# Linear attention into a gated feed-forward layer, one core: first batch's queries by chunk, tail numerators in column halves, PSUM banks from a table, a new order

## The chip, the cores and the metric

The kernel runs on one core of a Trainium2 chip. What counts is the device time of one execution in microseconds (us). Smaller is better.

## What is computed

The reference, cut to what matters:

```python
batch, n_heads, seq, head_dim = (8, 8, 576, 64); d_feat = 128
def phi(x):
    proj = np.einsum('bhsd,df->bhsf', x, w_phi)
    proj = proj - np.max(np.abs(proj), axis=-1, keepdims=True)
    return np.concatenate([np.exp(proj), np.exp(-proj)], axis=-1)
q_p, k_p = (phi(q), phi(k))
kv = np.einsum('bhsf,bhsd->bhfd', k_p, v)
z = np.sum(k_p, axis=2)
num = np.einsum('bhsf,bhfd->bhsd', q_p, kv)
den = np.einsum('bhsf,bhf->bhs', q_p, z)[..., None] + 1e-06
x = (num / den) as [4608 tokens, 512]
gate = np.maximum(x @ w_gate, 0.0); val = x @ w_val      # [512, 1536]
out = gate * val @ w_out                                   # [1536, 512]
```

## The kernel before

**The pieces.** A batch has 576 tokens and 8 heads. The first 512 tokens of a batch are its main part, four chunks of 128. The last 64 are its tail, and the tails of two batches that follow each other share one tile of 128 rows (a unit "u", four in all). The feed-forward layer then runs in nine groups of 512 tokens: one for each batch's main part (0 to 7) and one for the tails (8).

**Keys.** A key tile is turned (head_dim into the partitions), for batches 0 and 1 by TensorE with a copy (`kT`, `kTc`), later by a transposing DMA on SyncE's queue (`turn`). TensorE multiplies it with `w_phi` in two halves of 64 rows that sit in the two halves of the array (`rows_of`, L312). VectorE takes the largest magnitude (`km`, L319), ScalarE the two exponentials (`ke`, L368) and the factor of the row (`kk`, L379), and GpSimd or VectorE scales the values by it (`vs`, L328). TensorE then sums over tokens (`kv`, L486, and L509 for batches 0 and 1), and a copy brings the result to SBUF (`kvc`, L422).

**Queries.** The projection is made twice: with features in the partitions for the exponentials (`qc`, L549, then `qe`, L567), and with tokens in the partitions for the row maximum (`qr`, L312, then `qm`). From them come the numerators and denominators, three groups of heads for each chunk: `n` on TensorE (L597), `nt` (L616) and `nu` (L628) on VectorE, the reciprocal and the division (`xu`, L635 and L642, the latter on GpSimd unless the order says otherwise). The result is turned into `xT` by TensorE and a copy (`xT`, `xc`, L662) for batches 0 and 1, by a DMA after that (`xd`, L650).

For a tail unit, the numerators are made once with the first batch's `kv` and once with the second's, each time for all 128 rows and into a PSUM bank of its own. VectorE then reads 64 rows of each, so that `nt` and `nu` are two instructions of 64 rows each.

**Feed-forward.** One step makes 128 hidden columns for 512 tokens: four matmuls for the value (`fv`, L734) and a copy (L749), four for the gate (`fg`, L734), and VectorE's product of the two (L756). Twelve steps make `h`, then `fo` (L791) multiplies by `w_out`, a copy (L805) and a store follow. Group 0 starts before its batch is complete: its first four hidden blocks are made by halves of 256 tokens (`FIRST`), each with a bank, a copy and a product of its own.

**The order.** Every piece is an "atom" that registers itself with a number. `ORDER` lists all numbers, and `run` issues them in that order; an accent after a number takes the other engine (`alt`), and `zN` puts in N matmuls of zeros. Instructions of one engine run in the order in which they are issued, so the string sets each engine's own order and that of the queues on which GpSimd and SyncE issue DMAs. The eight PSUM banks come from one pool of eight buffers, taken in turn. `val_sb` has four buffers, `h2` one.

Of the kernel before, what the change touches and what calls it, by code (L numbers as in the profile page):

```python
# [11 lines left out]
ALU = mybir.AluOpType  # L12
# [4 lines left out]

K_CUTS = [[4, 8, 16, 24, 32], [8, 16, 24, 32]]
# [5 lines left out]


ORDER = """7 z3 82 92 93 83' 84 87 94 86 8 0 98 102 85 89 90 91 88 103 z1 104 96 97 108 105 95 107 106 z1 112
113 109 99 101 110' 111 122 114 115 123' 124 127 118 116 132 1 117 133 119 120 121 125 100' 128 z1
148 149 129 126 187 10 134 188 151 153 155 137 2 131 156 135 158 160 142 130 196 144 136 200 198
150 154 236 139 141 237 143 140 246 247 157 159 152 29 161 162 226 190 192 54 138 256 257 175 163
194 176 164 165 189 145 147' 191 266 177 146 3 267 193 4 169 170 166 167 171 168 195 199 181 178  # L30
182 321 214 5 172 179 183 180 184 201 197 217 215 11 220 221 218 222 219 208 9 322' 216 173 174'
282 283 223 209 185 186' 202 203 238 227' 210 205 206 204 207 240 211 1092 1093 1094 224 225' 239
1095 1096 324 328 228 229 242 212 213' 1097 326 232 1098 1099 1100 1101 1102' 231 6 1103 1104 1105
1106 1107 230 241 1108 243 268 269 270 271 273 258 274 272 261 248 251 260 249 253 255 254 1109 252
259 263 39 1110' 1111 1112' 264 1113 1114 275 250 233 1115 1116' 1117 290 361 262 363 265 292 365
279 280' 281' 323 327 291 295 293 1118 1119 294 1120' 1121 284 325 288 330 30 51 332 334 234 245
244 235 276 277 329 333 285 287 13 40 278' 289 1122 1123 351 296 1124 335 352 353 309 312 310 311
# [3 lines left out]
347' 32 55 61 371 372 307 308' 16 1134 63 388 398 402 399 391 400 383 385 1135' 1136 389 1137 401  # L41
42 403 1138' 405 393 367 368 369 395 392 394 390 1139 1140 1141 33 1142' 1143 1144' 17 43 424 426
428 384 418 454 458 420 1145 456 1146' 422 1147 1148 460 462 464 465 419 421 423 508 512 509 1149
# [4 lines left out]
502 1163 1164 1165' 534 536 538 564 529 531 523 1166 1167 568 503 570 476 574 566 533 569 571 1168  # L48
573 515 514 516 572 18 1169 1170 535 517 539 528 537 530 488 491 524 492 525 526 527 532 1171' 1172
1173 1174 1175 489 563 66 67 565 20 45 504 34 505 506 69 19 44 1176 1177 493 36 1178' 495 1179 567  # L50
507' 1180' 1181 494 490 590 555 496 497 1182' 593 575 591 68 587 588 589 540 1183 592 594 541 542
# [3 lines left out]
585 586 643 1199 1200 46 72 657 661 659 646 650 647 616 619 1201' 608 648 618 649 651 652 609 1202  # L55
# [3 lines left out]
675 676 716 717 741 1217 672 673 677 718 719 704 705 706 707 708 709 47 1218' 1219 1220 1221 1222  # L59
669 670 721 722 723 671 1223 1224 674 720 724 740 615 1225 1226 683 684 685 756 757 725 746 747 749  # L60
53 766 770 768 678 679 743 759 1227 1228 750 1229 1230' 710 711 712 760 713 758 761 763 714 680 681
# [58 lines left out]
def kernel(  # L120
# [594 lines left out]
    for b in range(B):  # L715
# [3 lines left out]
        if b % 2 == 1:  # L719
            q_tails(b // 2)  # L720


    t_count = [0]

    def ffn(g):
        st = {}
# [137 lines left out]
```

## Time and profile before

| | |
|---|---|
| three runs | 379.0, 384.38 and 378.77 us, median 379.0 |
| profiled execution, first to last instruction | 377.4 us |
| TensorE (PE) busy | 368.1 us, 98% |
| VectorE (DVE) busy | 290.7 us, 77% |
| ScalarE (ACT) busy | 213.1 us, 56% |
| GpSimd (POOL) busy | 151.3 us, 40% |
| granted TensorE clock, mean | 0.995 |

The profile tells of one execution. PE rows are matmuls, PEld rows weight loads. In a timeline row stand the start, the length from the first start to the last end, the engine, the line, what is written and read, and the count. One matmul's own length is its latency (about 0.38 us for 512 columns): the next one starts long before that has passed, so the rate is read from distances between starts. A line of the stretches (windows) has the bounds, the length, the busy time and count of each engine, the granted clock, the DMA engines' share and the rate.

### The profile page before, as it was taken

The numbers are of one execution on the slowest core, as the hardware profiler recorded it, in microseconds if no ns is written. First come the engines' busy times: TensorE is split into PE (matmuls) and PEld (weight loads), VectorE is DVE, ScalarE is ACT, GpSimd is POOL, SyncE is SP. The second block draws the span as 40 slices with busy tenths as digits, with TensorE's granted clock in tenths as the row PEclk, the third lists the DMA queues.
The fourth block names the chain that finished last, engine by engine and source line by source line (L and its number), as shares of the span: only waits on it lengthen the run. The fifth ranks groups of instructions, "written<-read, shape, count | busy, mean of one in ns | idle before, by whom it ended". The sixth has DMA issues, their size and how long they took to land.

```text
span 377.4 us, 8960 instructions
## 1 busy us (share of the span) xinstructions
PE 368.1 (98%) x3502; PEld 197.4 (52%) x3502; DVE 290.7 (77%) x633; ACT 213.1 (56%) x509; POOL 151.3 (40%) x201
## 2 busy tenths in 40 slices
PE   7789999999999999999999999999999999999996
PEld 4568465546545555464554554465455444444443
DVE  6998999988876799888868886988768927824641
ACT  6997888877687556876765359882740302111101
POOL 5883672488275275901842126933700210000000
PEclk9899999999999999999999999999999999999999
DMA  8999999999489959781289678620410130021004
GB/s 260 205 200 215 233 131 174 219 172 137 89 213 236 165 67 171 144 182 28 59 160 179 96 174 132 130 16 16 128 41 2 29 113 29 2 67 58 2 2 109
DMA packets 87929, 45.10 MB, mean 120 GB/s; under 512 B 55824, under 2 KB 82000, under 8 KB 87888
## 3 DMA queue, kind: packets, MB, share of 16 engines
q1 hardware_dynamic: 60208, 30.42, 37.3%
q0 software_dynamic: 27200, 13.57, 28.8%
q8 instruction: 27, 0.44, 0.5%
q10 hardware_dynamic: 480, 0.56, 0.5%
q14 instruction: 14, 0.11, 0.1%
HBM read 37.78 MB, written 9.44 MB: 125 GB/s over the span
## 4 chain that ended last, share of the span: by engine, by line
PE 92%; ACT 3%; DMA 3%; issue 0%; SPq 0%; DVE 0%; POOL 0%; DVEq 0%
PE pa L734 49%; PE pa L791 25%; PE pa L597 5%; PE pa L312 5%; PE pa L486 4%; PE pa L549 2%; DMA qn<-in_q_dram 2%; ACT qp L567 2%; PE pa L271 1%; PE pa L509 1%; DMA vn<-in_k_dram 1%; ACT kp L368 1%; ACT kv L422 0%; ACT val_sb L749 0%; ACT xT L662 0%
## 5 line engine op out<-in xcount | busy, mean ns | idle before, releaser
L791 PE MATMUL pa<-wo_sb,h 128*128 128x512 bf16 (+2 forms) x444 | 99.9, 373 | 0.0
L734 PE MATMUL pa<-xT,wv_sb 128*128 128x512 bf16 (+1 forms) x400 | 99.3, 370 | 0.1
L734 PE MATMUL pa<-xT,wg_sb 128*128 128x512 bf16 (+1 forms) x400 | 99.3, 370 | 0.0
L756 DVE SCALAR_TENSOR_TENSOR h<-pa,val_sb 128x512 bf16<-128x512 f32 (+1 forms) x112 | 74.6, 669 | 27.2 <-PE pa L734 20.5
L749 ACT CAST val_sb<-pa 128x512 bf16<-128x512 f32 (+1 forms) x67 | 38.1, 575 | 97.1 <-PE pa L734 88.0
L567 ACT ACTIVATE qp<-pa 128x512 bf16<-128x512 f32 x144 | 76.2, 618 | 15.1 <-PE pa L549 14.8
L368 ACT ACTIVATE kp<-pa 128x512 bf16<-128x512 f32 (+1 forms) x152 | 77.4, 605 | 11.1 <-PE pa L312 9.8
L328 POOL TENSOR_TENSOR vs<-vn,ek 128x512 bf16<-128x512 f32 (+1 forms) x68 | 67.4, 1005 | 31.1 <-DMA vn<-in_v_dram 15.2
L734 PEld LDWEIGHTS <-wv_sb 128*128 128x128 bf16 x448 | 41.9, 98 | 44.9 <-issue 1.2
L734 PEld LDWEIGHTS <-wg_sb 128*128 128x128 bf16 x448 | 41.6, 98 | 43.5 <-issue 0.7
L791 PEld LDWEIGHTS <-h 128*128 128x128 bf16 x444 | 40.8, 98 | 44.6 <-issue 0.8
L319 DVE TENSOR_REDUCE mq<-pa 128x4 f32<-128x512 f32 x72 | 46.5, 683 | 10.4 <-PE pa L312 10.1
L319 DVE TENSOR_REDUCE mk<-pa 128x4 f32<-128x512 f32 (+1 forms) x76 | 47.8, 653 | 3.9 <-ACT kp L368 2.3
L642 POOL TENSOR_TENSOR xu<-u,r 128x512 bf16<-128x512 f32 x22 | 22.8, 1041 | 67.4 <-DVE r L635 53.5
L642 POOL TENSOR_TENSOR tT<-u,r 128x512 bf16<-128x512 f32 x14 | 14.6, 1042 | 73.0 <-DVE r L635 41.0
L628 DVE TENSOR_TENSOR u<-pa,t 128x195 f32<-128x195 f32 (+3 forms) x120 | 38.2, 333 | 3.3
L616 DVE TENSOR_TENSOR t<-pa,cq 128x195 f32<-128x195 f32 (+3 forms) x120 | 36.8, 325 | 2.2 <-PE pa L597 1.0
L597 PEld LDWEIGHTS <-qp 128*128 128x128 bf16 x640 | 28.1, 98 | 14.0 <-ACT qp L567 0.9
L749 DVE CAST val_sb<-pa 128x512 bf16<-128x512 f32 (+1 forms) x45 | 30.7, 682 | 4.5 <-PE pa L734 3.0
L597 PE MATMUL pa<-kv,qp 128*128 128x65 bf16 x640 | 31.0, 193 | 0.9 <-ACT qp L567 0.5
L805 DVE COPY out_sb<-pa 128x512 f32<-128x512 f32 x13 | 8.9, 688 | 13.8 <-PE pa L791 13.6
L486 PEld LDWEIGHTS <-kp 128*128 128x128 bf16 x480 | 16.6, 98 | 3.9 <-issue 0.7
(71 smaller groups left out, 278.4 us busy)
## 6 DMA issues: line engine op xcount, KB each, us to landing
vn<-in_v_dram SPq DMA_DIRECT2D x6, 1024.0 KB, 7.3
qn<-in_q_dram POOLq DMA_DIRECT2D x8, 512.0 KB, 8.6
out_dram<-tT SPq DMA_DIRECT2D x16, 256.0 KB, 2.9
out_dram<-out_sb SPq DMA_DIRECT2D x16, 256.0 KB, 2.9
kn<-in_k_dram POOLq DMA_DIRECT2D x6, 512.0 KB, 9.1
wv_sb<-in_moe_w_val_dram POOLq DMA_DIRECT2D x3, 512.0 KB, 10.2
wg_sb<-in_moe_w_gate_dram POOLq DMA_DIRECT2D x3, 512.0 KB, 9.1
wo_sb<-in_moe_w_out_dram POOLq DMA_DIRECT2D x1, 1536.0 KB, 19.5
```

What stands on the lines that cost most here:

```text
L319: nc.vector.tensor_reduce(m, some.rearrange("p (c f) -> p c f", f=F), axis=AX.X, op=ALU.max, apply_absolute_value=True,)
L328: eng.tensor_tensor(dst[:, :, s, 0:D], src, ek[:, :, s : s + 1].to_broadcast(list(src.shape)), op=ALU.mult,)
L368: nc.scalar.activation(st["kp"][:, s, 0 : n // 2, par, :], st["banks"][par][:, 0 : n // 2 * F].rearrange("p (a f) -> p a f", f=F), AF.Exp, ...
L567: nc.scalar.activation(x["qp"][:, s, slot].rearrange("p a b -> p (a b)"), st["cols", i][par], AF.Exp, scale=sign,)
L597: nc.tensor.matmul(pn[:, E * (2 * i + s) : E * (2 * i + s + 1)], lhsT=x["qp"][:, s, slot, blk, :], rhs=kv_of(b, lo + i)[:, s, :],)
L616: nc.vector.tensor_tensor(x["t", j][rows, 0:n], ab[:, :, 1], c[:, :, None].to_broadcast([np_, n, E]), op=ALU.mult,)
L628: nc.vector.tensor_tensor(x["u"][rows, lo : lo + n], ab[:, :, 0], x["t", j][rows, 0:n], op=ALU.add)
L642: copy_of(alt, nc.gpsimd, nc.vector).tensor_tensor(x["xu"], x["u"][:, :, 0:D], x["r"].to_broadcast([P, H, D]), op=ALU.mult)
L734: nc.tensor.matmul(ps, lhsT=w[:, dc, P * fi : P * fi + P], rhs=xTs[g][:, dc, lo:hi], start=(dc == 0), stop=(dc == NDC - 1),)
L749: copy_by(copy_of(alt, "ACT", "DVE"))(st["val", n], ps)
L756: nc.vector.scalar_tensor_tensor(st["h2"][:, fi, lo:hi], ps, 0.0, st["val", n], op0=ALU.max, op1=ALU.mult)
L791: nc.tensor.matmul(po, lhsT=st["h2"][:, fi, P * t : P * t + P], rhs=wo_sb[:, fi, c0:c1], start=(fi == 0), stop=(fi == NFC - 1),)
```

## The change

The diff touches the following:

- `bank()` takes each PSUM tile from the bank that the next digit of a string `BANKS` names, in place of a pool of eight in turn.
- `SPLIT`: for the two query items of batch 0, the atoms `qc`, `qr` and `qk` are split by parity, which is by chunk: each half projects, and takes its factors, for one chunk.
- `KV_LAST`: the `kv` sums of batch 0 come in two atoms, the second with the last four blocks of tokens.
- Tail numerators: for the first batch of a unit only columns 0 to 63 of the weights are loaded and rows 0 to 63 of the bank written, for the second 64 to 127. Both land in one bank. `nt` and `nu` become one instruction of 128 rows each.
- Group 0's first hidden blocks: two blocks of 256 tokens share a bank, a copy and a product.
- `out_tile` and the buffer of `xu` are chosen by tile number instead of by a running count.
- `ORDER` is a new string (first words below), and so is the use of the accents in it.
- `PLAIN`, `TWICE` are empty, `Q_TURN` and `X_TURN` equal the old `TURN`: code for them is there and not used.

```diff
+SPLIT = {(0, 0), (0, 1)}
+KV_LAST = {0: 4}
-ORDER = """7 z3 82 92 93 83' 84 87 94 86 8 0 98 102 85 89 90 91 88 103 z1 104 96 97 108 105 95 107 106 z1 112
+ORDER = """z3 82 83 z1 84 92 87 102 86 88 93 7 85 94 8 0 103' 1 z1 104 97 89 98 95 122 112 105 107 123 29 124
...
+BANKS = """70712345 67703214 67365220 47563206 13206540 71236057 34120573 41672403 61075165 30176250 43143510
...
-    ps_a = ctx.enter_context(tc.tile_pool(name="ps_a", bufs=8, space=bass.MemoryType.PSUM))
+    ps_a = ctx.enter_context(tc.tile_pool(name="ps_a", bufs=1, space=bass.MemoryType.PSUM))
     def bank(dtype=FP32):
-        return ps_a.tile([P, 512 if dtype == FP32 else 1024], dtype, name="pa", tag="pa")
+        tag = f"pa{next(places)}"
+        return ps_a.tile([P, 512 if dtype == FP32 else 1024], dtype, name="pa", tag=tag)
...
+        last = [x for x in order if x[2] >= 2 * CP * (part + 1) - KV_LAST.get(b, 0)]
+        order = [x for x in order if x not in last] + last
+        cuts = [0, len(order) - len(last), len(order)]
+        for piece, (lo, hi) in enumerate(zip(cuts, cuts[1:])):
...
+            @atoms.add("kv", b, part, piece)
...
+            for pars in ((0,), (1,)) if split else ((0, 1),):
+                at = (i, *pars) if split else (i,)
+
+                @atoms.add("qc", *key, *at)
+                def _(alt, i=i, pars=pars):
+                    for par in pars:
+                        st["cols", i, par] = bank()
...
+                @atoms.add("qr", *key, *at)
+                def _(alt, i=i, pars=pars):
+                    for par in pars:
+                        st["rows", i, par] = bank()
+                    rows_of(T4(i), {par: st["rows", i, par] for par in pars})
...
+        for ci in range(len(chunks) if split else 1):
+
+            @atoms.add("qk", *key, *((ci,) if split else ()))
...
-                    for bi, b in enumerate(batches):
-                        pn = x["pn", j, bi] = bank()
-                        for i in range(n):
-                            slot, blk = place(lo + i)
-                            for s in range(2):
+                    pn = x["pn", j] = bank()
+                    for i in range(n):
+                        slot, blk = place(lo + i)
+                        for s in range(2):
+                            for bi, b in enumerate(batches):
+                                rows = slice(np_ * bi, np_ * (bi + 1))
                                 nc.tensor.matmul(
-                                    pn[:, E * (2 * i + s) : E * (2 * i + s + 1)],
-                                    lhsT=x["qp"][:, s, slot, blk, :],
+                                    pn[rows, E * (2 * i + s) : E * (2 * i + s + 1)],
+                                    lhsT=x["qp"][:, s, slot, blk, rows],
                                     rhs=kv_of(b, lo + i)[:, s, :],
                                 )
...
-            steps = [(fi, P * lo, P * hi) for lo, hi, f0, f1 in FIRST for fi in range(f0, f1)]
+            steps = [
+                (fi, C // (hi - lo), P * lo, P * hi)
+                for lo, hi, f0, f1 in FIRST
+                for fi in range(f0, f1, C // (hi - lo))
+            ]
...
+        def half_step(fi, nf, w, lo, hi):
+            ps = bank().rearrange("p (f n) -> p f n", f=nf)
+            for i in range(nf):
+                for dc in range(NDC):
+                    nc.tensor.matmul(
+                        ps[:, i],
+                        lhsT=w[:, dc, P * (fi + i) : P * (fi + i + 1)],
+                        rhs=xTs[g][:, dc, lo:hi],
```

How the new string moves instructions is shown at three places. In these rows stand the line, the operation, what is written and read with the tile's name (some with a running number), and the written shape; lines of the changed kernel have other numbers.

**PE, numerators of a tail unit.** `qp` holds a unit's exponentials, each `kv` one batch's sums for two heads. Before:

```order
L734 MATMUL pa_1800<-xT_1628,wv_sb_94 128x512
L597 LDWEIGHTS qp_1526
L597 MATMUL pa_1813<-kv_467,qp_1526 128x65
L597 LDWEIGHTS qp_1526
L597 MATMUL pa_1813<-kv_467,qp_1526 128x65
L597 LDWEIGHTS qp_1526
L597 MATMUL pa_1813<-kv_440,qp_1526 128x65
```

and now:

```order
L302 MATMUL pa_1684<-ident0_98,xu_1648 128x128
L688 LDWEIGHTS qp_1471
L688 MATMUL pa_1689<-kv_480,qp_1471 64x65
L688 LDWEIGHTS qp_1471
L688 MATMUL pa_1689<-kv_1374,qp_1471 64x65
L688 LDWEIGHTS qp_1471
L688 MATMUL pa_1689<-kv_480,qp_1471 64x65
```

The two batches of the unit now alternate, each with 64 rows of the same bank; there are 128 such matmuls for 128 of the old. In the old order the twelve groups of them stand in the middle of other full-array work; in the new one they stand in six runs.

**POOL, the loads behind the first batch.** `vs` are scaled values, `qm` and `km` the tails' queries and keys, `wg_sb`, `wv_sb`, `wo_sb` the weights, `kn` here batch 2's keys, `xu` the divided numerators of batch 0. Before:

```order
L328 TENSOR_TENSOR vs<-vn_109,ek 128x4x64
L236 DMA qm<-in_q_dram 64x8x64 x2
L243 DMA wg_sb<-in_moe_w_gate_dram 128x4x512
L243 DMA wv_sb<-in_moe_w_val_dram 128x4x512
L243 DMA wg_sb<-in_moe_w_gate_dram 128x4x512
L642 TENSOR_TENSOR xu<-u,r 128x512 x2
L214 DMA kn<-in_k_dram 128x8x256
L642 TENSOR_TENSOR xu<-u,r 128x512 x2
L252 DMA wo_sb<-in_moe_w_out_dram 128x12x512
```

and now (the `qm` pair stands much further ahead, shown in the second piece):

```order
L274 DMA wg_sb<-in_moe_w_gate_dram 128x4x512
L274 DMA wv_sb<-in_moe_w_val_dram 128x4x512
L274 DMA wg_sb<-in_moe_w_gate_dram 128x4x512
L283 DMA wo_sb<-in_moe_w_out_dram 128x12x512
L245 DMA kn<-in_k_dram 128x8x256
L728 TENSOR_TENSOR xu<-u,r 128x512 x2
L267 DMA km<-in_k_dram 64x8x64 x2
L728 TENSOR_TENSOR xu<-u,r 128x512 x2
```

```order
L251 DMA kn<-in_k_dram 128x4x576
L274 DMA wv_sb<-in_moe_w_val_dram 128x4x512
L274 DMA wg_sb<-in_moe_w_gate_dram 128x4x512
L267 DMA qm<-in_q_dram 64x8x64 x2
L361 TENSOR_TENSOR vs<-vn_109,ek 128x4x64
```

The output weights have gone ahead of batch 2's keys, the tails' queries ahead of every other value of batch 0, and the tails' keys between the two pairs of divisions.

**DVE, just ahead of the first product of the feed-forward layer.** `t` and `u` are the steps of the numerators, `r` the reciprocal, `mk` and `mq` row maxima, `tT` and `xT` turned tiles, `h` the hidden tile. Before:

```order
L284 COPY tT_761<-pa 128x1024
L635 RECIPROCAL r<-u 128x8
L616 TENSOR_TENSOR t<-pa,cq 128x130
L616 TENSOR_TENSOR t<-pa,cq 128x195
L628 TENSOR_TENSOR u<-pa,t 128x130
L616 TENSOR_TENSOR t<-pa,cq 128x195
L628 TENSOR_TENSOR u<-pa,t 128x195 x2
L635 RECIPROCAL r<-u 128x8
L756 SCALAR_TENSOR_TENSOR h_823<-pa,val_sb 128x256
L319 TENSOR_REDUCE mk<-pa 128x4
```

and now:

```order
L748 COPY xT<-pa 128x4x128
L722 RECIPROCAL r<-u 128x8
L701 TENSOR_TENSOR t<-pa,cq 128x195
L701 TENSOR_TENSOR t<-pa,cq 128x130
L712 TENSOR_TENSOR u<-pa,t 128x130
L712 TENSOR_TENSOR u<-pa,t 128x195 x2
L722 RECIPROCAL r<-u 128x8
L315 COPY tT_846<-pa 128x1024
L352 TENSOR_REDUCE mk<-pa 128x4
L847 SCALAR_TENSOR_TENSOR h_850<-pa,val_sb 128x2x256
L352 TENSOR_REDUCE mk<-pa 128x4
```

The copies of the first two turned chunks have come from ACT to DVE, one maximum of batch 1 stands ahead of the first product, and that product has 512 columns instead of 256.

More of the change, by code (lines that the diff above doesn't have):

```diff
@@ L284, in turned_copy @@
         copy_by(by)(st["T"].rearrange("p a b -> p (a b)"), st["pt"][:, 0 : n * P])
-    for b in range(TURN, B):
-        for n in "kq":
+    for b in range(min(TURN, Q_TURN), B):
+        for n, first in (("k", TURN), ("q", Q_TURN)):
+            if b < first:
+                continue
             @atoms.add("turn", n, b)
@@ L310, in rows_of @@
         for j in range(T.shape[1]):
-            for par in range(2):
+            for par in banks:
                 nc.tensor.matmul(
@@ L351, in _ @@
                 st["T"] = T()
-            st["banks"] = [bank(), bank()]
+            st["banks"] = {par: bank() for par in range(2)}
             rows_of(st["T"], st["banks"])
+        twice = key in TWICE
+        if twice:
+            @atoms.add("kx", *key)
+            def _(alt):
+                st["again"] = {par: bank() for par in range(2)}
+                rows_of(st["T"], st["again"])
         for par in range(2):
@@ L521 @@
     GROUPS = ((0, 3), (3, 3), (6, 2))
-    x_count = [0]
     def q_item(key, groups, T, chunks, by_dma, blocks=None):
         st, xs = {}, [{} for _ in chunks]
+        split = key in SPLIT
         width = 8 * len(groups)
@@ L720 @@
             q_tails(b // 2)
[L723 removed]
     def ffn(g):
         st = {}
[L727 removed]
+        steps = [(fi, 1, 0, SF) for fi in range(NFC)]
         if g == 0:
[L729 to L749 removed]
+            steps = [
+                (fi, C // (hi - lo), P * lo, P * hi)
+                for lo, hi, f0, f1 in FIRST
+                for fi in range(f0, f1, C // (hi - lo))
+            ]
@@ L751, in _ @@
+        for n, (fi, nf, lo, hi) in enumerate(steps):
+            @atoms.add("fv", g, n)
+            def _(alt, n=n, fi=fi, nf=nf, lo=lo, hi=hi):
+                ps = half_step(fi, nf, wv_sb, lo, hi)
+                st["val", n] = sb_g.tile([P, SF], BF16, name="val_sb")
+                copy_by(copy_of(alt, "ACT", "DVE"))(
+                    st["val", n], ps.rearrange("p f n -> p (f n)")
+                )
             @atoms.add("fg", g, n)
-            def _(alt, n=n, fi=fi, lo=lo, hi=hi):
+            def _(alt, n=n, fi=fi, nf=nf, lo=lo, hi=hi):
```

285 lines of the change are left out of this document (148 added, 137 removed), and 52 rows, old and new, of tables (BANKS, ORDER).

## The prediction

> **What bounds the kernel now.** First the page's span, its busy shares and the chain that ended last, then the stretches (start and length, busy time and count of PE, PEld, DVE, ACT and POOL, granted clock, DMA share, GB/s).
>
> ```profile
> span 377.4 us, 8960 instructions
> PE 368.1 (98%) x3502; PEld 197.4 (52%) x3502; DVE 290.7 (77%) x633; ACT 213.1 (56%) x509; POOL 151.3 (40%) x201
> PE 92%; ACT 3%; DMA 3%; issue 0%; SPq 0%; DVE 0%; POOL 0%; DVEq 0%
> ```
> ```profile
> 5.00:10.00 5.00, 4.36 (x26) 2.83 (x22) 3.73 (x8) 4.46 (x17) 2.74 (x5) 1.00 1.11 340
> 10.00:15.00 5.00, 3.76 (x45) 2.65 (x47) 4.87 (x10) 4.94 (x18) 4.49 (x7) 0.77 1.30 204
> 15.00:20.00 5.00, 4.22 (x112) 2.93 (x106) 4.77 (x10) 4.59 (x14) 4.21 (x8) 0.88 1.25 206
> 20.00:25.00 5.00, 4.68 (x131) 3.64 (x130) 4.96 (x16) 4.75 (x13) 4.93 (x8) 1.00 1.36 201
> 25.00:30.00 5.00, 4.36 (x71) 3.49 (x68) 4.91 (x20) 4.82 (x11) 3.98 (x4) 1.00 1.43 201
> 35.00:40.00 5.00, 5.00 (x53) 3.50 (x52) 4.54 (x11) 3.22 (x13) 0.00 (x0) 1.00 1.18 298
> 350.00:360.00 10.00, 10.00 (x48) 4.55 (x47) 5.80 (x10) 1.75 (x3) 0.00 (x0) 1.00 0.01 2
> ```
>
> Three stages. Up to about 30 us DVE and ACT work without a break (from 10 us on 4.6 to 5.0 of every 5) and PE is only nominally busy: 288 matmuls from 10 to 25 us, most of them of 65 or 128 columns. From 35 us PE is busy all the time. A busy PE need not run at its rate, so I read the distances between starts in the timeline:
>
> ```profile
> 62.89 0.66 PE L597 MATMUL pa<-kv,qp 128*128 128x65 bf16 x16
> 63.39 1.89 PE L791 MATMUL pa<-wo_sb,h 128*128 128x512 bf16 x8
> 69.63 1.03 PE L791 MATMUL pa<-wo_sb,h 128*128 128x512 bf16 x4
> 70.59 0.62 PE L312 MATMUL pa<-w,kT 64*128 64x128 bf16 x16
> 71.14 1.04 PE L791 MATMUL pa<-wo_sb,h 128*128 128x512 bf16 x4
> 72.02 1.03 PE L734 MATMUL pa<-xT,wv_sb 128*128 128x512 bf16 x4
> 72.88 1.03 PE L734 MATMUL pa<-xT,wg_sb 128*128 128x512 bf16 x4
> ```
>
> From 72.02 to 72.88 four matmuls of 512 columns take 0.86 us, 0.215 each. The stretch 350 to 360 has 48 of them or parts of them, the same rate. Sixteen numerator matmuls of 65 columns take 0.50 us (62.89 to 63.39), 31 ns each. What is not at that pace is the step between full-array matmuls (128\*128) and those in half arrays (64\*128): 69.63 to 70.59 is 0.96 us for four, 0.10 over. Sixteen half-array matmuls then take 0.55 us; the eight pairs stand 0.056 us apart where they run on, 0.45 together, so the way back costs 0.10 too. Beyond these steps I find no PE wait from 40 us on. Counting each matmul at its start distance (1252 of 512 columns at 0.2155 us make 270 of it), PE's list needs 348.7 us, of which 14.0 stand ahead of the first feed-forward matmul. That one starts at 28.91 (row below), 14.9 us behind; PE ends at 373.7 (367.71 + 6.02), 25.0 behind. The 64 switches of array shape after the first 500 matmuls, 6.4 us, are most of what is added in between. Last comes a tail of about 3.7 us: copy, store, close.
>
> ```profile
> 367.71 6.02 PE L791 MATMUL pa<-wo_sb,h 128*128 128x512 bf16 x39
> 368.56 0.59 ACT L805 COPY out_sb<-pa 128x512 f32<-128x512 f32 x1 [8.91 <-PE pa L791]
> 371.15 0.69 DVE L805 COPY tT<-pa 128x512 f32<-128x512 f32 x1 [4.49 <-PE pa L791]
> 374.19 0.61 ACTq L776 DMA_DIRECT2D out_dram<-u  x1
> ```
>
> So time can be won or lost in four ways: PE's own work, the start, the tail, and new waits of PE.
>
> **Column halves.** 128 tail matmuls now use half the columns each, two batches in turn. The nearest row is the other kind of half array, the sums of batch 0 (pairs in two row halves, also 65 columns):
>
> ```profile
> 21.80 1.27 PE L509 MATMUL pa<-vs,kp 64*128 64x65 bf16 x72
> 28.04 0.34 PE L597 MATMUL pa<-kv,qp 128*128 128x65 bf16 x6
> ```
>
> 72 of them in 1.27 us with the last one's 0.19 is 15 ns each, against 31 for the full array. If column halves overlap as row halves do, 128 × (31 − 15) = 2.0 us go; if they don't, nothing. I take **−2.0** (bounds −2.0 and 0), since the pair reads the same rows and writes one bank in different partitions, as near to that row as any.
>
> **Switches of array shape.** Counted along PE's built order the shape changes 86 times before and 102 times now. Past the first 500 matmuls, where PE is the bound, it is 64 and 76, and all twelve more are the ways into and out of the six runs of column halves. At 0.10 us each: **+1.2**. No row shows a column switch: free it would be 0, at twice the row price +2.4. The Trainium skill, "TensorEngine Tiling (Array Packing)", Tiling Modes, Key Properties, says that a change of tiling mode drains the engine while a change of tile within the mode does not; by that every one of the twelve costs, and the 0.10 at each change above agrees. Column halves and their switches together are then worth −0.8 us, which is the whole gain in PE's own work: the multiset of all other matmuls is unchanged.
>
> **VectorE and ScalarE.** The halved tail rows take 24 instructions from DVE:
>
> ```profile
> L616 DVE TENSOR_TENSOR t<-pa,cq 64x195 f32<-64x195 f32 x16 | 5.7, 354 | 0.3
> ```
>
> The 16 of 195 columns, the 8 of 130, and as many of the next step (`u`) become half as many, some 8 us less; merged copies and products of group 0 take 4 + 4 instructions more away. All of that but the group-0 part lies after 50 us, where DVE has a fifth of its time free and PE none: **0**. It would count only if DVE held PE, which no stretch after 35 us shows.
>
> **The start.** The same multiset of matmuls stands on PE ahead of the first feed-forward matmul in both orders, so the start moves only with the engines that bind it. Start distances and the first events:
>
> ```profile
> 10.94 1.88 DVE L319 TENSOR_REDUCE mk<-pa 128x4 f32<-128x512 f32 x3
> 10.72 2.06 ACT L368 ACTIVATE kp<-pa 128x512 bf16<-128x512 f32 x4
> 28.91 0.60 PE L734 MATMUL pa<-xT,wv_sb 128*128 128x256 bf16 x4
> 30.20 0.67 ACT L749 CAST val_sb<-pa 128x256 bf16<-128x256 f32 x2
> 30.63 0.43 DVE L756 SCALAR_TENSOR_TENSOR h<-pa,val_sb 128x256 bf16<-128x256 f32 x1 [0.38 <-PE pa L271]
> ```
>
> One more DVE instruction of 512 columns costs 0.60 us ((1.88 − 0.68) / 2), one on ACT 0.48 ((2.06 − 0.61) / 3). With these and the like for the smaller shapes, what ACT has ahead of the first value copy sums to 23.2 us before and 22.9 now; what DVE has ahead of the first product to 24.9 and 26.0. Before, they came 7.0 and 5.7 us behind their sums, mostly while waiting for the first loads, which are the same. So ACT copies at 29.9, and DVE multiplies at 31.7 instead of 30.6. The second turned chunk is now copied by DVE, behind 23.0 us of work, at 28.7 to 29.0, so PE starts its first feed-forward matmul at 29.2, not 28.9. The late product frees its bank late, but PE has two value steps (1.7 us) to do first. Splitting Q by chunk and `kv` in pieces lets PE start each sooner, and PE is not what binds here. I take **+0.2**. Bounds: DVE's idle time from 5 to 30 us is 1.8 us (1.27 + 0.13 + 0.23 + 0.04 + 0.09), so −1.8; the two tail-key loads of 0.7 us that POOL now issues between the divisions, if they hold up the last two chunks, +1.5.
>
> **The tail.** The last thirds of three tiles now end within two steps of 0.86 us; before, their copies were 2.6 us apart (368.56, 371.15). Three stores of 256 KB crowd before the last two small ones: **+0.2** (0 to +0.8). **New waits of PE** in 340 us of an order that is new throughout, with each bank now fixed beforehand (a bank that is still being read stops PE): **+0.3** (0 to +3). A step of 0.86 us needs one bank, and DVE and ACT free one each in 0.60 and 0.48, so the mean load leaves room.
>
> Sum: 377.4 − 2.0 + 1.2 + 0.2 + 0.2 + 0.3 = 377.3 for the profiled execution. The median of the runs stands 1.6 us over it (379.0), so **378.9 us**, no change that can be told: about 2%, 7.6 us, is what a measurement of this kernel separates from none.
>
> **Rival 1, slower: batch 2's keys come late.** The loads that POOL issues follow one another at about 200 GB/s (the stretches), and the output weights now go ahead of batch 2's keys.
>
> ```profile
> L214 POOL DMA_DIRECT2D kn<-in_k_dram x1: 952/952/952, 27.4 to 27.4; - x1
> DMA to landing us min/median/max: 14.8/14.8/14.8
> ```
> ```profile
> L252 POOL DMA_DIRECT2D wo_sb<-in_moe_w_out_dram x1: 1071/1071/1071, 31.4 to 31.4; - x1
> DMA to landing us min/median/max: 19.5/19.5/19.5
> ```
> ```profile
> L312 PE MATMUL pa<-w,kT x16: 216/216/227, 60.1 to 65.6; 64*128 64x128 bf16 x16
> L292 SPq DMA_TRANSPOSE kT<-kn x2: 3739/4660/5582, 42.2 to 65.9; - x2
> DMA to landing us min/median/max: 6.7/9.3/11.9
> ```
> ```profile
> L312 PE MATMUL pa<-w,kmT x8: 216/216/216, 65.7 to 65.8; 64*128 64x128 bf16 x8
> DMA to landing us min/median/max: 8.9/8.9/8.9
> ```
> ```profile
> SPq L298 <- DMA qm<-in_q_dram: 23.6, 1, 23.6
> ```
>
> Before, the keys landed at 42.2 and the weights at 50.9. The bytes are the same, so now the keys land at about 50.9. SP then issues the transposing DMA, 5.6 us long; landing after at most 11.9 us gives 62.8. The tail keys' one, behind it on SP, starts at 56.5 and lands 8.9 us later, at 65.4. PE's order now has 16 more output matmuls and 32 numerators ahead of the first `kT` matmul, 4.5 us, which puts it at 64.6, and the `kmT` ones stay at 65.7. So it fits by 1.8 and 0.3 us. For it: no slack; PE runs in order, so all feed-forward work queues behind these eight-matmul groups and stops. Against: with the tails' queries loaded earlier SP no longer waits 23.6 us for them, batch 1's values start earlier and are out of the way. If the keys land 5 us later, the price is 4.7 us, **383.6 us**; it decides for slower by 2% from keys that land about 8 us late, at 59.
>
> **Rival 2, column halves don't overlap.** Only the −2.0 falls away while the twelve switches stay: **380.9 us**. For it: no row of the trace has two column halves; each changes its weights, as all 65-column matmuls do. Against: the 15 ns of the row halves, where weights change each time too. The Trainium skill speaks for it: by "TensorEngine Tiling (Array Packing)", Restrictions and Gotchas, column tiling excludes the fast weight load, so loading weights could set the pace; no row here shows a load in that mode.
>
> **Rival 3, faster.** The first loads no longer idle DVE and the split Q closes its other gaps: 1.8 us less, no +0.2, no new waits, **376.6 us**. For it: that idle time exists. Against: in the two largest gaps DVE waits for PE's turned tiles, which wait for loads that are issued as before.
>
> ```profile
> DVE tT L284 <- PE pa L271: 1.5, 2, 0.9
> ```
>
> To reach 2% more than half of the 14.9 us start would have to go, of which DVE and ACT fill most.
>
> That the change does nothing it says (halved tail numerators aside) is my forecast for the split Q, the `kv` pieces and the banks, not a rival.
>
> **Numbers.** Forecast as summed 0.52 (its own range 377 to 381), rival 2 0.18, rival 1 0.14 (a third of it over 2%), rival 3 0.16 (a quarter of it over 2%, with whatever I don't see). Faster by 2% 0.04, within 0.89, slower 0.07. The range reaches from a start without DVE gaps and free switches (378.9 − 2.0 − 1.2 = 375.7) to keys nearly 5 us late, 383.5.
>
> **What will show it.** Tail numerators in the timeline: pairs at 15 ns against 31. Twelve column switches at 0.10. First feed-forward matmul near 29.2, first product near 31.7. A PE wait at the first `kT` or `kmT` matmul between 60 and 70 us would be rival 1. It is wrong if PE starts its feed-forward work before 27 us or after 32, or waits over 3 us in sum after 40 us.

## The result, and the profile after

The changed kernel takes **384.8 us** (median of four runs, 383.0 to 385.4) against 379.3 us of the kernel before: 1.0126 times as long, with a 95% interval of 1.0085 to 1.0167 (this ratio, like those below, is estimated from the single runs; the two medians alone give 1.0145). The prediction was 378.9 us, 375.7 to 383.5. The change is slower by an amount that can be told from none, though not by 2%.

The page of the changed kernel, profiled in its run of 385.4 us:

```profile
span 383.6 us, 8913 instructions
PE 369.4 (96%) x3502; PEld 195.2 (51%) x3502; DVE 278.1 (72%) x601; ACT 222.9 (58%) x528; POOL 142.5 (37%) x188
PE 89%; ACT 4%; DMA 2%; issue 2%; DVE 2%; POOL 0%; POOLq 0%
```

PE is busy as long as before (369.4 against 368.1 us) in a span 6.2 us longer, and "issue" and DVE, which had nothing in the chain before, have 2% each. The waits of PE from 28 us on (what waited, for what, in sum, times, longest):

```profile
PE pa L688 <- issue: 2.0, 1, 2.0
PE pa L345 <- DVE tT L898: 1.9, 1, 1.9
PE pa L823 <- DMA xT<-xu: 0.7, 1, 0.7
```

The same view of the kernel before has no row at all. The first wait stands in the middle of a group of numerators (timeline of PE; in brackets the idle time ahead of a row and what ended it):

```profile
50.97 2.35 PE L592 MATMUL pa<-vs,kp 64*128 64x65 bf16 x144
...
53.70 1.04 PE L823 MATMUL pa<-xT,wg_sb 128*128 128x512 bf16 x4
54.57 0.41 PE L688 MATMUL pa<-kv,qp 128*128 128x65 bf16 x8
57.00 0.41 PE L688 MATMUL pa<-kv,qp 128*128 128x65 bf16 x8 [2.01 <-issue]
57.25 1.52 PE L823 MATMUL pa<-xT,wv_sb 128*128 128x512 bf16 x4
58.55 1.92 PE L823 MATMUL pa<-xT,wg_sb 128*128 128x512 bf16 x4
```

Nothing of the profile releases PE at 57.00: "issue". It is the ninth of a chunk's sixteen numerators, in the middle of a group of six, with the inputs and the bank of the matmuls before it. And what follows is slow: from 58.55 to 60.26 four matmuls of 512 columns take 0.43 us each, twice 0.215. The stretches (start and end, length, busy time and count of PE, PEld, DVE, ACT, POOL, granted clock, DMA share, GB/s) say why:

```profile
55.00:57.00 2.00, 0.00 (x1) 0.00 (x1) 0.47 (x1) 0.00 (x0) 0.00 (x0) 1.00 0.88 54
57.00:58.00 1.00, 1.00 (x11) 0.59 (x11) 0.67 (x2) 0.00 (x0) 0.00 (x0) 0.82 0.75 212
58.00:59.00 1.00, 1.00 (x4) 0.32 (x3) 0.96 (x4) 0.36 (x2) 0.00 (x0) 0.50 0.96 276
59.00:60.00 1.00, 1.00 (x4) 0.44 (x3) 0.35 (x2) 1.00 (x3) 0.00 (x0) 0.50 0.99 311
60.00:61.00 1.00, 1.00 (x8) 0.46 (x6) 0.42 (x1) 1.00 (x3) 0.00 (x0) 0.50 1.14 306
61.00:62.00 1.00, 1.00 (x11) 0.54 (x10) 0.73 (x3) 0.41 (x1) 0.00 (x0) 0.97 1.96 202
```

The granted clock is 0.50 behind the idle time, until 61 us: 0.18 + 3 × 0.50 + 0.03 = 1.7 us lost on top of the 2.0. The second wait, in time order over the engines concerned:

```profile
235.07 3.51 POOL L361 TENSOR_TENSOR vs<-vn,ek 128x512 bf16<-128x512 f32 x3
235.59 3.06 DVE L457 CAST vsm<-ek 64x16 bf16<-64x16 f32 x1
...
237.26 0.22 PE L345 MATMUL pa<-w,kT 64*128 64x128 bf16 x1
238.53 0.24 POOL L488 CAST vs<-ek 128x16 bf16<-128x16 f32 x1
238.67 0.69 DVE L898 COPY tT<-pa 128x512 f32<-128x512 f32 x1
...
239.42 0.38 PE L345 MATMUL pa<-w,kT 64*128 64x128 bf16 x7 [1.94 <-DVE tT L898]
```

VectorE sits 3.06 us in a cast of 64 by 16 numbers (GpSimd's rows of the same cast take 0.25). Its copy of an output tile therefore runs at 238.7 and not at 235.7, the bank that the next key projection is given comes free late, and PE stands 1.9 us.

To see where the 6.2 us come from, I give each matmul its own floor, that is its start distance where PE runs on, as in the prediction (the column halves still at the 31 ns of the full array), and read how far PE lies behind this list at the same point of it:

| us of the list done | 30 | 45 | 130 | 140 | 210 | 220 | 340 |
|---|---|---|---|---|---|---|---|
| before, behind by | 15.9 | 16.8 | 20.0 | 20.5 | 22.7 | 23.2 | 24.9 |
| after, behind by | 15.5 | 20.1 | 22.9 | 24.2 | 26.7 | 29.5 | 30.7 |
| difference | -0.4 | +3.3 | +2.9 | +3.7 | +4.0 | +6.3 | +5.8 |

Three steps: +3.7 us at the first wait, +0.8 at the third (155 us), +2.3 at the second. Everything between them is as before or a little better.

### The profile page after: what moved, and what is told of

Same layout as the page of the kernel before. It is cut to its first block, busy times and chain, and to the rows that moved or that the text cites. A ratio compares the mean times of both kernels' runs of the same rounds, so it can differ in the third digit from the quotient of the medians.

```text
span 383.6 us, 8913 instructions
## 1 busy us (share of the span) xinstructions
PE 369.4 (96%) x3502; PEld 195.2 (51%) x3502; DVE 278.1 (72%) x601; ACT 222.9 (58%) x528; POOL 142.5 (37%) x188
## 4 chain that ended last, share of the span: by engine, by line
PE 89%; ACT 4%; DMA 2%; issue 2%; DVE 2%; POOL 0%; POOLq 0%
PE pa L823 49%; PE pa L884 22%; PE pa L688 5%; PE pa L345 4%; PE pa L560 4%; PE pa L634 2%; ACT kp L427 2%; PE pa L302 2%; DMA xT<-xu 2%; ACT qp L653 1%; PE pa L592 1%; DVE vsm L457 1%; DMA vn<-in_k_dram 1%; DVE vsm L361 1%; ACT ek L441 0%
## 5 line engine op out<-in xcount | busy, mean ns | idle before, releaser
L847 DVE SCALAR_TENSOR_TENSOR h<-pa,val_sb 128x512 bf16<-128x512 f32 x108 | 74.1, 688 | 36.2 <-PE pa L823 34.3
L823 PE MATMUL pa<-xT,wv_sb 128*128 128x512 bf16 (+1 forms) x400 | 95.4, 372 | 0.7 <-DMA xT<-xu 0.7
L838 ACT CAST val_sb<-pa 128x512 bf16<-128x512 f32 x74 | 44.2, 602 | 85.6 <-PE pa L823 85.3
L838 DVE CAST val_sb<-pa 128x512 bf16<-128x512 f32 x34 | 23.4, 688 | 20.7 <-PE pa L823 20.4
L701 DVE TENSOR_TENSOR t<-pa,cq 128x195 f32<-128x195 f32 (+1 forms) x108 | 32.8, 328 | 6.6 <-PE pa L688 6.3
L688 PEld LDWEIGHTS <-qp 128*128 128x128 bf16 (+1 forms) x640 | 26.8, 101 | 17.9 <-issue 5.4
L712 DVE TENSOR_TENSOR u<-pa,t 128x195 f32<-128x195 f32 (+1 forms) x108 | 32.9, 329 | 1.4
L688 PE MATMUL pa<-kv,qp 128*128 128x65 bf16 (+1 forms) x640 | 30.8, 195 | 2.1 <-issue 2.0
L728 POOL TENSOR_TENSOR tT<-u,r 128x512 bf16<-128x512 f32 x9 | 9.3, 1038 | 52.0 <-DVE r L722 47.7
L898 ACT COPY out_sb<-pa 128x512 f32<-128x512 f32 x12 | 7.2, 601 | 23.8 <-PE pa L884 23.8
```

What stands on the lines that cost most here:

```text
L688: nc.tensor.matmul(pn[rows, E * (2 * i + s) : E * (2 * i + s + 1)], lhsT=x["qp"][:, s, slot, blk, rows], rhs=kv_of(b, lo + i)[:, s, :],)
L701: nc.vector.tensor_tensor(x["t", j][:, 0:n], sums(x, j, n)[:, :, 1], c[:, :, None].to_broadcast([P, n, E]), op=ALU.mult,)
L712: nc.vector.tensor_tensor(x["u"][:, lo : lo + n], sums(x, j, n)[:, :, 0], x["t", j][:, 0:n], op=ALU.add,)
L728: copy_of(alt, nc.gpsimd, nc.vector).tensor_tensor(x["xu"], x["u"][:, :, 0:D], x["r"].to_broadcast([P, H, D]), op=ALU.mult)
L823: nc.tensor.matmul(ps[:, i], lhsT=w[:, dc, P * (fi + i) : P * (fi + i + 1)], rhs=xTs[g][:, dc, lo:hi], start=(dc == 0), stop=(dc == NDC - 1),)
L838: copy_by(copy_of(alt, "ACT", "DVE"))(st["val", n], ps.rearrange("p f n -> p (f n)"))
```

## The experiments

**Theory of the first wait: PE's own program comes too late.** The profile's DMA queues hold one that carries instructions in packets of 16 KB (a block of the program; below, its transfer is a refill):

```profile
q8 instruction: 27, 0.44, 0.5%
```

27 packets for 7,018 PE instructions is one for 256. The trace has another short gap without a releaser, 0.52 us at 20.83 us. Counted along PE's built order the two gaps stand ahead of numbers 432 and 1456, 1,024 apart, that is 4 × 256; so I set the block ends at 256k - 80 (the 80 are fitted, for what runs ahead of the kernel). A packet then starts some us after PE has gone into a new block. By the theory it is for the block after that one: two blocks are held at a time, and one that PE runs through faster than a refill takes ends in idle time. In the new order the two sums of batch 1 (72 small matmuls each, 144 instructions with their weight loads) stand side by side; the block from 1200 to 1456 is done in 3.2 us (51.55 to 54.79). Before, the sums were 5.6 us apart, and it took 7.8 us:

```profile
47.43 1.25 PE L509 MATMUL pa<-vs,kp 64*128 64x65 bf16 x72
...
53.06 1.26 PE L509 MATMUL pa<-vs,kp 64*128 64x65 bf16 x72
```

The rivals: the wait is for data or a bank that the profile does not show; or the block's speed is harmless and the turning DMAs of batch 2's keys, in flight from 49.9 to 57 us, hold the packet up.

**Shift the block ends.** 92 small matmuls of zeros where PE waits for the first queries:

```diff
-    def keep_busy(n):
+    def keep_busy(n, pad=0):
+        for i in range(pad):
+            nc.tensor.matmul(scratch[D * (i % 2) : D * (i % 2 + 1), 0:65],
+                             lhsT=zeros[:, D * (i % 2) : D * (i % 2 + 1)], rhs=zeros[:, 0:65])
```

> The changed kernel with one addition: 92 small matmuls of zeros (184 PE instructions with their weight loads, about 1.5 us) while PE waits for the first queries at 11.4 to 12.7 us. Everything behind keeps its order, data and banks; only its running number on PE grows by 184. Refill theory (PE's program comes in blocks of 256 instructions, a block is asked for when the last but one is finished and is there about 5.4 us later; the block in which both sums of batch 1 stand takes 3.4 us): the block ends fall elsewhere, the idle 2.0 us at 55 us go, and the halved clock behind them; about 381.0. A gap of up to 1 us near 17 to 22 us, where 256 instructions take 4.3 us, stays or moves. Rival, late data or a bank at that numerator: 2.0 us idle at the same matmul (the ninth of its eight-head group), 384.8. Rival, the turning DMAs hold the refill up: it goes as well, so this run does not tell that one apart.

```profile
21.07 0.33 PE L597 MATMUL pa<-vs,kp 64*128 64x65 bf16 x10
24.16 0.27 PE L597 MATMUL pa<-vs,kp 64*128 64x65 bf16 x6 [2.76 <-issue]
...
54.76 2.35 PE L597 MATMUL pa<-vs,kp 64*128 64x65 bf16 x144
56.95 0.39 PE L350 MATMUL pa<-w,tT 64*128 64x128 bf16 x8
57.17 0.38 PE L639 MATMUL pa<-qmT,w 64*128 64x512 bf16 x2
57.48 0.82 PE L828 MATMUL pa<-xT,wg_sb 128*128 128x512 bf16 x2
```

The gap behind the batch 1 sums is gone with the same data, banks and DMAs, so the rival of late data falls. But a gap of 2.76 us now stands at 24.16, in the sums of batch 0, where I had allowed 1 us: it is number 688 of this kernel's count, a block end again. The first feed-forward matmul came 3.8 us later (32.5 us) and the time did not fall (386.4 us, 1.017 of before, 1.010 to 1.025). In this profile the granted clock is 0.50 twice: from 25 to 28 us behind the new gap, and from 240 to 243 us behind the second wait, which is 1.9 us here too. The mechanism came out as expected, the price did not.

**Set the two sums apart.** Same data and DMAs, 12 feed-forward matmuls and a projection between them (the diff with the atoms' names in place of their numbers; some banks change with it):

```diff
-fg.0.8 fg.0.3 vs.1.1.1 fg.0.9 qr.1.0.0 ... kv.1.1.0 kvc.1.1.0' qe.1.0.0.1 kv.1.0.0
+fg.0.8 kv.1.1.0 fg.0.3 vs.1.1.1 fg.0.9 kvc.1.1.0' kvc.1.1.1 qr.1.0.0 ... qe.1.0.0.1 kv.1.0.0
```

> The changed kernel with the sums of batch 1's second half moved ahead, behind the feed-forward step before, so that 12 feed-forward matmuls' worth of time (1.7 us) and a projection (0.45 us) lie between the two groups of 72 small matmuls; two other banks for it, nothing else. Refill theory: the block of 256 instructions takes about 5.4 us in place of 3.4, the idle 2.0 us at 55 us shrink to 0.3 or less, the clock stays whole; about 381.0. Rival, the turning DMAs (at the same time as before): 2.0 us stay, 384.8. Rival, late data or a bank at the numerators: 2.0 us stay, 384.8.

```profile
PE pa L344 <- DVE tT L897: 1.9, 1, 1.9
PE pa L344 <- DVE kv L495: 1.2, 1, 1.2
PE pa L883 <- issue: 1.0, 6, 0.2
PE pa L591 <- DVE mq L351: 0.2, 1, 0.2
```

The gap is gone (the block takes 6.9 us, PE goes on 0.03 us after its end), the clock stays 1.00. Two new waits of my own making take 1.4 us back in this profile: 1.2 us for a copy of the sums that I had put behind a product, and 0.2 us for a maximum, each holding a bank. (The six "issue" rows of 0.16 us are no waits: this profile holds records of 3,451 of the 3,502 matmuls, and the rows stand where a weight load has a record and its matmul has none. The same six stand in five other runs, which lack 51 records too.) 383.9 us, 1.0123 of before (1.0036 to 1.0209). So the fast block is needed for the gap; that was the point, and 381 was missed.

**Copy the keys plainly instead of turning them** (batch 2's and the second tails', which then stay unturned):

```diff
-                nc.sync.dma_start_transpose(out=t, in_=flat)
+                nc.sync.dma_start(out=t.rearrange("p a b -> p (a b)"), in_=flat)
```

> The changed kernel with batch 2's keys and the second tails' keys copied by a plain DMA of the same bytes in place of the turning DMA, so these keys are not turned; order, banks and all waits as they were. Rival, the turning DMAs hold the refill up: the idle 2.0 us at 55 us go, 381.0. Refill theory without them: the block still runs in 3.4 us, at least 1 us of the gap stays (only the packet's own 1.2 us and a part of the 2.9 us ahead of it can shrink). Late data or a bank: 2.0 us stay.

```profile
54.72 0.41 PE L694 MATMUL pa<-kv,qp 128*128 128x65 bf16 x8
55.78 0.41 PE L694 MATMUL pa<-kv,qp 128*128 128x65 bf16 x8 [0.65 <-issue]
```

One run, 382.2 us. Most of the gap goes, not all, and less stays than the 1 us that I took as the least without the rival. By this one run both have a part; it is taken up again below.

**Let ScalarE make the small cast.**

```diff
-                eng.tensor_copy(dst[:, :, :, D], ek)
+                copy_of(alt, eng.tensor_copy, nc.scalar.copy)(dst[:, :, :, D], ek)
```

> The changed kernel with one small cast (64 partitions by 16, the last tails' values) made by ScalarE in place of VectorE, where it took 3.06 us from 235.6 while GpSimd multiplied. Theory (VectorE stood still in that cast because GpSimd worked on SBUF, so the copy of an output tile, its bank and PE came late): the cast takes 0.2 to 0.3 us on ScalarE, the copy runs at about 235.7, the 1.9 us idle of PE at 239 go; 382.4 to 382.9. Rival, the fixed bank itself is at fault: the idle stays at 1 us or more, 384 to 385. The idle 2.0 us at 55 us stay in both.

```profile
231.82 0.26 ACT L457 CAST vsm<-ek 64x16 bf16<-64x16 f32 x1
...
232.31 3.51 POOL L361 TENSOR_TENSOR vs<-vn,ek 128x512 bf16<-128x512 f32 x3
232.93 0.69 DVE L898 COPY tT<-pa 128x512 f32<-128x512 f32 x1
...
234.49 0.39 PE L345 MATMUL pa<-w,kT 64*128 64x128 bf16 x8
```

As expected: 0.26 us on ScalarE, the copy from PSUM runs beside the same three multiplications of GpSimd, no wait of PE. 381.7 us, 1.0068 of before (1.0028 to 1.0108), 3.1 us less than the changed kernel: more than the 1.9 us of the wait and the 0.2 us around it. The third wait is not in this profile either, but the cast did not cause it: it stands 80 us ahead of the cast, and it is absent from the run with the sums apart and from the burst below, which both keep the cast. What sets it stays open. So for the second wait the fixed bank was only where it showed; the cause was VectorE's cast. In the changed kernel it ended at 238.65, 0.07 us after the third multiplication (235.07 + 3.51 = 238.58). The Trainium skill, "SBUF — State Buffer", says that a pair of ports is shared by the two engines as an exclusive lock, held for a whole instruction, for VectorE's fast two-port copies out of SBUF among others. These two runs agree that VectorE stands while GpSimd works, but the cast stood through three multiplications in a row, from inside the first to the end of the third, and not to the end of one instruction. Whether it is such a copy, and why it stood so long, no run here shows.

**The sums side by side in the kernel before**, alone:

```diff
-... kv.1.1 kvc.1.1.0' kvc.1.1.1' qc.1.1.0 ... vs.1.0.1 kv.1.0 ...
+... qc.1.1.0 ... vs.1.0.1 kv.1.1 kvc.1.1.0' kvc.1.1.1' kv.1.0 ...
```

> The kernel before, with one move: the sums of batch 1's second half (72 small matmuls, 144 PE instructions) come directly ahead of those of the first half instead of 5.6 us earlier, as they stand in the changed kernel. Refill theory: the block of 256 instructions from number 1200 to 1456 then takes about 4.9 us; with a refill of 5.4 us (the changed kernel) to 7.1 us (the same packet in the kernel before) PE must stand idle 0.5 to 2.2 us at number 1456 with nothing to release it, and go on 1.3 to 1.5 us after the end of the packet; 379.7 to 381.4, and 1.7 more in runs in which the clock halves. Rival, the table of banks or late data of the changed kernel: no such idle here, 379.2.

```profile
52.85 2.35 PE L508 MATMUL pa<-vs,kp 64*128 64x65 bf16 x144
55.05 0.38 PE L548 MATMUL pa<-tT,w 64*128 64x512 bf16 x2
55.27 0.39 PE L311 MATMUL pa<-w,tT 64*128 64x128 bf16 x8
55.58 1.04 PE L733 MATMUL pa<-xT,wv_sb 128*128 128x512 bf16 x4
56.46 1.03 PE L733 MATMUL pa<-xT,wg_sb 128*128 128x512 bf16 x4
57.32 0.35 PE L596 MATMUL pa<-kv,qp 128*128 128x65 bf16 x6
```

No gap, 379.8 us (0.9934 to 1.0014): missed. The block took 4.0 us, less than I had worked out, but the packet came 1.1 us after PE entered it, not 3.96 as in the kernel before, and the refill was there just then. The turning DMA of batch 2's keys was near its end by then (issued at 42.9, landed at 55.4); before, PE entered the block at 48.7, in the middle of it. Side by side is not enough; the refill must be slow at that moment too.

**The refill by itself**: 288 zero matmuls in column halves in the last group, where the queues are nearly idle (`z0p288` ahead of one value step).

> The changed kernel with 288 extra small matmuls of zeros in column halves (576 PE instructions with their weight loads, 4.3 us at 15 ns a matmul) in the last group, where the DMA queues carry next to nothing: the refill measured by itself. Refill theory: a block of 256 of these takes 1.9 us, and even with idle queues a refill takes the packet's 0.9 us, 1.3 to 1.5 us behind it and the request; so PE stands idle 0.4 to 2 us at each of two block ends, 256 instructions apart, and goes on 1.3 to 1.5 us after the packet's end. Rival, the refill is slow only beside the turning DMAs: no gap, 4.3 us in one piece.

```profile
q8 instruction: 29, 0.48, 0.5%
```
```profile
359.11 4.27 PE L230 MATMUL pa<-zeros 128*64 128x65 bf16 x257
364.09 0.67 PE L230 MATMUL pa<-zeros 128*64 128x65 bf16 x31 [0.71 <-issue]
```

One gap, not two: the block that the burst begins with had been fetched long before. Two packets more for 576 instructions more ties the queue to PE. Together (times in us; blocks counted as above; the lower rows had no gap):

| kernel, block end | PE enters the block | packet starts, lasts | PE's last of the block, next | packet's end to next |
|---|---|---|---|---|
| after, 432 | 16.13 | 18.52, 0.95 | 20.12, 20.83 | 1.37 |
| after, 1456 | 51.55 | 54.41, 1.18 | 54.79, 57.00 | 1.40 |
| zeros at the start, 688 | 17.70 | 21.70, 1.06 | 21.21, 24.16 | 1.41 |
| plain copies, 1456 | 51.70 | 53.48, 0.99 | 54.94, 55.78 | 1.30 |
| cast on ScalarE, 1456 | 51.34 | 53.92, 1.17 | 54.58, 56.52 | 1.42 |
| burst, 7344 | 361.16 | 361.74, 0.94 | 363.18, 364.09 | 1.40 |
| before, 1456 | 48.73 | 52.70, 1.73 | 56.50, 56.53 | 2.10 |
| side by side, 1456 | 53.43 | 54.53, 1.37 | 57.38, 57.41 | 1.51 |

Each time that PE stood, it went on 1.3 to 1.5 us after its packet had ended. A refill from entering a block takes 2.9 us with idle queues (361.16 to 364.09), 5.4 at 55 us in the changed kernel and 6.5 with the zeros at the start (17.70 to 24.16); in the kernel before it would have been 7.1 (3.96 + 1.73 + 1.4) for a block that lasted 7.8. The Trainium skill, "Runtime: NRT & Kernel Launch", Instruction fetch mechanics, has the 256 instructions and the 16 KB, and that this is hidden because instructions go out more slowly than a block fills; here small matmuls go out faster (256 instructions in 2.0 us in the burst), and it is not hidden. The measurement decides.

**What the turning DMAs add**: both edits, cast on ScalarE and plain copies, so that these keys stay unturned here too.

> The changed kernel with the small cast on ScalarE and with batch 2's keys and the second tails' keys copied plainly in place of turned (these keys are then not turned), order and banks as changed. Against the run with the cast alone (381.7 median, idle of PE at the block end 1.9 us in its profile) it tells what the turning DMAs add to the refill: if they hold the request up, the packet comes 1 to 1.8 us after the request instead of 2.1 to 2.9, the idle is 0.3 to 1.0 us, the clock does not halve in any run, 380.0 to 380.6. If they don't: idle 1.4 to 2.2 us, 381.7, some runs at 384.

```profile
PE pa L694 <- issue: 0.9, 1, 0.9
```

The gap is 0.9 us in the wait view; 379.6 us, the ten runs from 379.1 to 381.4 and none at 384, as three of ten with the cast alone were. That is 2.1 us less than the cast alone and under the range that I gave. With the turning DMAs the packet starts 2.05, 2.58 and 2.86 us after PE enters the block (burst, cast alone, changed kernel) and lasts 1.08 to 1.18; with plain copies it is 1.78 and 2.02, and 0.99. So in these five executions they lengthen the refill, by 0.1 to 1.3 us. That is less than the 2.1 us. A halved clock is not the rest of it at the median: the cast alone's runs from 381.1 to 381.8 us have a mean clock of 0.999 or 1.0. What the rest is stays open.

**Column halves alone, in the kernel before.** The second bank is still taken, so that the turn of the banks stays:

```diff
-                    for bi, b in enumerate(batches):
-                        pn = x["pn", j, bi] = bank()
...
-                                    pn[:, E * (2 * i + s) : E * (2 * i + s + 1)],
-                                    lhsT=x["qp"][:, s, slot, blk, :],
+                                    pn[rows, E * (2 * i + s) : E * (2 * i + s + 1)],
+                                    lhsT=x["qp"][:, s, slot, blk, rows],
```

> The kernel before with the column halves alone (half the columns of the weights for each batch of a tail unit, both into one bank, one VectorE instruction in place of two; the second bank is still taken and left unused, so that the turn of the banks stays). The twelve groups stand alone among full-array work here, in place of six runs. Expected from the terms measured in the changed kernel: 128 times 14 to 16 ns less, up to 24 changes of the array's shape at 0.095 us more: -2.0 and +1.9 to +2.4, so 379.1 to 379.6. Rival, halves that don't overlap: +2.3, 381.5.

380.0 us, 0.9997 of before (0.9952 to 1.0042); the range that I gave, 379.1 to 379.6, went by 379.2 for the kernel before, which had a median of 379.8 beside this run. In its trace the halves overlap, 17 ns a matmul, and 24 changes of shape cost 94 ns on the way in and 112 on the way out, 2.5 us in sum: about as expected. Where the groups stand alone, the switches eat the gain.

**Both causes out.** The sums apart, with free banks and both copies on VectorE, and the cast on ScalarE; then twice with other banks for a few atoms, for waits that the edit itself had made.

> The changed kernel with both edits: the sums of batch 1's second half moved ahead behind one feed-forward step (this time with banks that are free by then and both copies on VectorE right behind, so that it adds no wait of its own), and the small cast on ScalarE. If the two causes found are the whole loss: no idle of PE over 0.5 us after 30 us; span 376 to 377, 377.6 to 378.6, that is 0.6 to 1.6 us under the kernel before: the 0.8 us that column halves save less their switches, a little better or worse at the start. If something else slows the changed kernel: 380 or more.

> The kernel with both edits once more, with other banks for nine atoms around the moved sums, so that neither the first half's sums nor the next gate step take a bank that VectorE is still reading a maximum from (0.9 and 0.7 us of idle PE in the run with both edits). If those two waits are all that was left: no idle of PE over 0.5 us after 30 us, 1.6 us less than the run with both edits, 379.0 to 379.6, no difference to the kernel before. If the column halves' 0.8 us and a start no worse come through as well: 378.0 to 378.9. If the time stays at 381, the loss is not in these waits.

> The kernel with both edits a last time, with other banks for three numerator atoms and one gate step, which took a bank just behind a reader and cost PE 0.5 us twice in the run before. If these were what was left: no idle of PE over 0.3 us after 30 us, 1.0 us less than that run's 380.8, so 379.6 to 380.0, no difference to the kernel before. If the changed kernel's better start (0.6 us) and its column halves (0.8 us) count in the time as well: 378.2 to 379.0. If it stays at 380.8, something is slower that PE's waits don't show.

381.0, 380.8 and 380.7 us, all three above what I expected; the last is 1.0034 of before (1.0014 to 1.0054). None has the gap. Each time the waits that I had aimed at went and others stood in their place: 1.8, 1.0 and 1.2 us in sum. Those of PE left in the last:

```profile
PE pa L883 <- DVE u L711: 0.8, 1, 0.8
PE pa L822 <- DMA xT<-xu: 0.4, 1, 0.4
```

These 1.2 us are near the 1.4 us to the kernel before, but the 0.8 us that the column halves should save don't show, and 0.8 us fewer waits from the first version to the second took only 0.3 us off; so something may be slower that PE's waits don't show, and that stays open. The two causes are 4 of the 5.5 us. With them gone the rest of the change gains nothing: the last version is still slower by 0.1 to 0.5%, and no version here beats the kernel before.

## Why the prediction was wrong

- **New waits of PE, +0.3 (0 to +3): the step that failed.** It measured about 7 us: 2.2 + 1.7 behind the sums of batch 1, 2.3 behind the cast, 0.8 for a turned tile. I priced it by the mean load of VectorE and ScalarE and by banks. The largest wait is not one for an engine at all, and the second came from a small cast that the prediction does not name: the order gave it to VectorE, where it took 3.06 us beside GpSimd's work, against 0.25 in GpSimd's rows. The mean load of an engine holds neither.
- **The trace of before held the sign.** PE's number 688 stands there at 27.66 us, 1.45 us after its packet's end, behind a gap of 0.3 us, and the block at 55 us had 0.7 us to spare. I looked for waits from 40 us on and for what releases them, and never counted PE's instructions against time.
- **Column halves, -2.0:** right. Thirty-two in a row:

```profile
151.50 0.70 PE L688 MATMUL pa<-kv,qp 128*64 128x65 bf16 x32
152.14 1.04 PE L884 MATMUL pa<-wo_sb,h 128*128 128x512 bf16 x4
```

  0.70 us with the last one's 0.19: 16 ns each against 31, so 1.9 us. Rival 2 falls: loading weights did not set the pace in this mode.
- **Switches, +1.2:** right. Six ways in at 93 ns (one 182) and six out at 113 make 1.3 us, with two row switches fewer 1.1.
- **Start, +0.2:** the first feed-forward matmul at 28.7 (29.2 forecast), the first product at 31.6 (31.7). At 30 us of its list PE is 0.4 us better than before, not 0.2 worse: a small miss inside the bounds.

```profile
28.72 1.91 PE L823 MATMUL pa<-xT,wv_sb 128*128 128x256 bf16 x16
31.62 0.69 DVE L847 SCALAR_TENSOR_TENSOR h<-pa,val_sb 128x512 bf16<-128x512 f32 x1
```

- **Tail, +0.2:** 4.0 us from PE's end to the span's, against 3.7: right. **VectorE, 0:** its 12.6 us less (290.7 to 278.1) bought nothing, as said; the one time that it held PE, in the cast, counts above.
- **Rival 1:** batch 2's keys were in time. Their turned tiles landed at 56.9 and 57.4; the first matmul that reads them runs at 68.5 and waits for nothing. Its time, 383.6, was near the result for another reason.
- **The range** ended at 383.5 on that rival. A wait bounded by 3 us in sum, plus a clock that halves behind it, should have carried it further.

## What to carry to other kernels

When an order changes, count the instructions of the engine that bounds against time, not only their durations: here 256 PE instructions that run faster than a refill (2.9 us with idle queues, 5.4 and 6.5 beside other transfers) can leave PE without a program, and groups of small matmuls are best kept apart, and away from heavy DMA. An idle row with "issue" in the middle of a uniform group is the sign, if no matmul record is missing there and it stands at a block end (here 256k - 80). Before a small VectorE copy between SBUF tiles is moved next to long GpSimd work, look at that work's length, not at the copy's.

## What the hardware did that I had not expected

- A refill of PE's program: 2.9 us with idle queues, 5.4 us beside the loads and turning DMAs at 55 us, 6.5 us at 18 to 24 us with the zeros at the start; always 1.3 to 1.5 us from the packet's end to the next instruction where PE stood waiting.
- The granted clock went to 0.50 for about 3.4 us after 2.0 us of idle PE in the changed kernel; after the idle 1.9 us at 239 us in the same execution it did not. In the run with zeros at the start it did, behind that very wait; and with the cast on ScalarE it stayed at 1.00 behind 1.9 us of idle PE at 55 us. So the length of the idle time alone does not tell.
- VectorE's cast of 64 by 16 took 3.06 us beside GpSimd, while its reads of PSUM beside the same work took their usual 0.69.
- A way out of column halves costs more than a way in: 112 against 94 ns, and 182 straight from row halves.
